# Attention and two dense layers on one core: the products of two pairs of heads in one run, and the keys' exponential one step earlier

## The chip, the cores and the metric

The kernel runs on one core of one Trainium2 chip. The metric is the device time of one execution in microseconds; the kernel before was run three times. One further execution was taken by the hardware profiler, and all rows shown below come from that one.

## The reference

All arithmetic is in fp32. Attention here has no score matrix: queries are normalized along the 64 features of a head, keys along the 576 positions, and the output is `softmax(q) @ (softmax(k)^T @ v)`, for 8 batches of 8 heads. Then come two dense layers over 4608 tokens.

```python
q_s = softmax(q, axis=-1)             # along the 64 features
k_s = softmax(k, axis=2)              # along the 576 positions
kv  = einsum('bhsd,bhse->bhde', k_s, v)     # 64 x 64 for each head
x   = einsum('bhsd,bhde->bhse', q_s, kv)    # then heads side by side: 4608 x 512
h   = x @ moe_w_in;  x = (h - tanh(h)) @ moe_w_out          # 512 -> 2048 -> 512
h   = x @ moe2_w_in; g = P(h) / (Q(h) + 1e-6)               # cubic over quadratic
out = g @ moe2_w_out
```

## The kernel before

**Blocks and steps.** The 4608 tokens are cut into nine blocks of 512 (`NB`). The first dense layer takes 16 steps a block (`KF`), 144 steps `n` in all. In a step TensorE (PE) makes `first_product`: 12 matmuls of 128x128 by 128x512 into a PSUM tile `hps`, and `second_product1` for the step two before: 12 matmuls into the four `acc` banks. Between the two stand a tanh (ACT, L947), `g = h - tanh(h)` (DVE, L950), and the split of `g` into a high part (ACT, L336) and a low part (POOL, L340). A second stage does the second dense layer after step 143, from about 898 us on; the change does not touch it.

**Attention rides along.** While block `j-1` is in the first dense layer, the attention of block `j` is made in small pieces that are put into the steps by hand. `put(s, fn, j, p)` hangs a piece on step `s`; `p` counts the four pairs of heads, and `first(j)` is the first step of block `j-1`. A plain function runs at the head of its step (`front`), ahead of `first_product`. A tuple of two runs in two places: the first function after the step's dense products (`turn`), the second after the split of `g` (`follow`). Batches have 576 positions and blocks 512, so keys and values of batch `b = j` are made for block `j`.

**Keys of one pair** (`KV_LATER`): `kv_max` and `kv_squares` (DVE: maximum over positions, a transposition, a second maximum, a small result `kd` sent to DRAM), `kv_fetch` (SP: `kd` back, broadcast to all partitions), `kv_join` (DVE, L539), `kv_sub` (DVE, L481), `kv_exp` (ACT, L491), `kv_mm` (PE, L499: 10 matmuls of 128x64 by 128x65, which the trace shows as 20 instructions), and `kv_norm`: `kv_sum` (DVE, L506 and L507) and `kv_parts` (ACT, L513: the result into `bd`).

**Queries of one pair** (`Q_LATER`): `q_max` (DVE, L570), `q_sub` (POOL), `q_exp` (ACT, L585), `q_sum` (DVE, L590 to L592, and POOL), `q_squares` (DVE, L610, and a DMA to DRAM), `q_fetch` (SP, L619: four DMAs back, transposed), `q_mm` (PE, L637: matmuls of 64x64, in two PSUM banks), and `q_out` (ACT, L649: four copies into `xr`). At the last step of a block `next_x` splits `xr` into `xh` (ACT, L320) and `xl` (DVE, L322) for the next block's `first_product`.

**Where the products lie.** Counted from `first(j)`, `q_mm` of the four pairs is at steps 4, 8, 11 and 14. `kv_mm` of pair `p` is at the step of `q_mm` of pair `p-1` and writes the free half of that pair's first bank (`room`); pair 0 is two steps ahead of the block, where the last `q_mm` of the block before is. So PE has four runs of attention products a block. Each pair's keys have `kv_join` and `kv_sub` one step ahead of `kv_mm`, and `kv_exp` at the head of the step of `kv_mm`.

**PSUM and buffers.** `ps_h` has two banks, both used in turn by `hps`; `ps_a` has two banks for the attention. In SBUF the pool `att` holds, by `LATER`, two buffers of `qr`, `qe`, `qm`, `qs` and `rs`, and one of everything else.

**Errands.** At the end of each step, after `follow`, generators advance by one piece: they prepare the second layer's weights (`errands`: ACT L131, L133 and L221, DVE, POOL, DMAs) and the first layer's result (`x2_units`: ACT L365, POOL, DMAs). They share ACT's and SP's queues with the attention.

Of the kernel before, what the change touches and what calls it, by code (L numbers as in the profile page):

```python
# [8 lines left out]
F32 = mybir.dt.float32  # L9
# [5 lines left out]
AF = mybir.ActivationFunctionType  # L15
# [3 lines left out]
P = 128  # L19
NB = 512  # L20
NEG = -3.0e38
EPS_S = 1e-9
# [21 lines left out]
def attention_moe_moe2_kernel(ctx, tc, q, k, v, w1, w2, w3, w4, ca, cb, out):  # L44
# [8 lines left out]
    B, H, S, D = q.shape  # L53
# [13 lines left out]
    bdp = tc.alloc_tile_pool(name="bdp", bufs=1, side="right")  # L67
# [122 lines left out]
    HALF = NB // 2  # L190
# [124 lines left out]
    xr = xp.tile([P, KC, NB], F32, tag="xr", name="xr")  # L315
# [39 lines left out]
    def x2_units(j, k0, k1, ta, tb, free):  # L355
# [35 lines left out]
    absb = const.tile([P, 2], F32, name="absb")  # L391

    bd = {
        (par, p): bdp.tile([P, 2, D], F32, tag=f"bd{par}{p}", name=f"bd{par}{p}")
        for par in range(2) for p in range(NPAIR)
    }
    HEADS = slice(0, D), slice(D, P)
    G = -(-S // P)
    REST = S - (G - 1) * P

    FIRST = {"qr": 4, "ke": 4, "qe": 4, "mx": 2, "mc": 2, "qm": 4, "qs": 4, "rs": 4, "qh": 2}
    LATER = {"qr": 2, "qe": 2, "qm": 2, "qs": 2, "rs": 2}
# [38 lines left out]
    kv_state = {}  # L441
# [47 lines left out]
    def kv_exp(b, p):  # L489
        e = kv_state[b, p]  # L490
        ACT.activation(out=e, in_=e, func=AF.Exp)  # L491

    def kv_mm(b, p, room=None):
        e, vs = kv_state.pop((b, p)), vt.pop((b, p))
        pool, tag = (ps_h, "h") if b == 0 and p >= 2 else (ps_a, "a")
        ps = pool.tile([P, NB], F32, tag=tag, name="kvps") if room is None else room
        for g in range(G):
            for h in range(2):
                PE.matmul(  # L499
                    ps[HEADS[h], HALF:HALF + D + 1], e[:, g, h, :], vs[:, h, g, :], start=g == 0, stop=g == G - 1  # L500
                )
        kv_state[b, p] = ps

    def kv_sum(b, p):
        rs = att_tile(b, [P, 1], F32, "rs")
        DVE.tensor_scalar_add(rs, kv_state[b, p][:, HALF + D:HALF + D + 1], EPS_S)  # L506
        DVE.reciprocal(rs, rs)  # L507
        kv_state[b, p] = kv_state[b, p], rs

    def kv_parts(b, p):  # L510
        ps, rs = kv_state.pop((b, p))
        for h, r in enumerate(HEADS):
            ACT.activation(out=bd[b % 2, p][r, h], in_=ps[r, HALF:HALF + D], func=AF.Copy, scale=rs[r])  # L513

    def kv_norm(b, p):
        kv_sum(b, p)
# [12 lines left out]

    def kv_fetch(b, p):  # L530
        d = kv_state[b, p].rearrange("p c -> (p c)")
        t = att_tile(b, [P, G, 2, D], F32, "ke").rearrange("p g h d -> p (g h d)")[:, 0:NB]
        SP.dma_start(out=t, in_=d.unsqueeze(0).to_broadcast([P, NB]))
        kv_state[b, p] = t

    def kv_join(b, p):
# [2 lines left out]
        DVE.tensor_reduce(out=mx.rearrange("p (c i) -> p c i", i=SQ), in_=rows, axis=AX.X, op=ALU.max)  # L539
        kv_state[b, p] = mx  # L540

    KV_LATER = (kv_max, kv_squares, kv_fetch, kv_join, kv_sub, kv_exp, (kv_mm, kv_norm))
    KV = (kv_max, (kv_turn, kv_top), (kv_back, kv_sub), kv_exp, (kv_mm, kv_norm))

    def spans(j):

        got = []
        at = j * NB
        while at < (j + 1) * NB:
            b = at // S  # L550
# [55 lines left out]

    def q_squares(j, p):
        e = q_state[j, p].rearrange("p g d -> p (g d)")
        t = att_tile(j, [P, 4, 2, D], F32, "qe").rearrange("p g h d -> p (g h d)")
        DVE.transpose(out=t, in_=e)  # L610
        d = dp.tile([P, NB], F32, tag=f"qd{j}{p}", name=f"qd{j}{p}")
        SP.dma_start(out=d, in_=t)
        q_state[j, p] = d
# [8 lines left out]
    def q_mm(j, p):  # L622
        t = q_state[j, p]
        if j == 0:
            ps = ps_acc.tile([P, NB], F32, tag=f"acc{p}", name="xps")
            for h, r in enumerate(HEADS):
                PE.matmul(ps[r], bd[0, p][:, h], t, start=True, stop=True)
            q_state[j, p] = ps
            return
        ps = [ps_a.tile([P, NB], F32, tag="a", name="xps") for _ in range(2)]  # L630
        for b, p0, p1 in sorted(spans(j), key=lambda x: x[2] - x[1]):
            for to in range(2):
                for h, r in enumerate(HEADS):
                    def cols(a):
                        return a.rearrange("x (g p) -> x g p", p=P)[:, :, p0:p1]

                    PE.matmul(  # L637
                        cols(ps[h][HEADS[to], 0:HALF]), bd[b % 2, p][r, h], cols(t[r, to * HALF:(to + 1) * HALF]),
                        start=True, stop=True,
                    )  # L640
        q_state[j, p] = ps
        return ps[0]

    def q_out(j, p):
        ps = q_state.pop((j, p))
        if j > 0:
            for to in range(2):
                for h, r in enumerate(HEADS):
                    ACT.copy(out=xr[r, p, to * HALF:(to + 1) * HALF], in_=ps[h][HEADS[to], 0:HALF])  # L649
        else:  # L650
            ACT.copy(out=xh[:, p, :], in_=ps)
            DVE.tensor_tensor(out=xl[:, p, :], in0=ps, in1=f32(xh[:, p, :]), op=ALU.subtract)
# [9 lines left out]
    def turn(todo):  # L662

        got, room = [], None
        for fn, args in todo:
            if isinstance(fn, tuple):
                room = fn[0](*args, *([room] if room is not None and fn[0] is kv_mm else []))
                got.append(lambda fn=fn, args=args: fn[1](*args))
        return got

# [8 lines left out]
    def put(s, fn, *args):  # L679
        work[max(s, 0)].append((fn, args))  # L680

    def first(j):
        return (j - 1) * KF

    kv_at = {(1, p): 3 * p + 3 for p in range(NPAIR)}
    q_at = {(1, p): (6, 9, 12, 14)[p] for p in range(NPAIR)}
    for j in range(2, NBLK):
        for p in range(NPAIR):
            q_at[j, p] = first(j) + (4, 8, 11, 14)[p]
            if j < B:  # L690
                kv_at[j, p] = q_at[j, p - 1] if p else first(j) - (2 if j > 2 else 0)
    q_from = {(j, p): 3 * p if j == 1 else at - 7 for (j, p), at in q_at.items()}
    for j in range(1, NBLK):
        for p in range(NPAIR):
            if j < B:
                for fn, s in zip(KV, (-3, -2, -1, 0, 0)) if j == 1 else zip(KV_LATER, (-4, -4, -2, -1, -1, 0, 0)):
                    put(kv_at[j, p] + s, fn, j, p)
            s = q_from[j, p]
            steps = (s - 1, s, s + 1, s + 2, s + 4, q_at[j, p]) if j == 1 else (s - 1, s, s + 1, s + 2, s + 3, s + 5, s + 7)
            for fn, s in zip(Q if j == 1 else Q_LATER, steps):  # L700
                put(s, fn, j, p)
        for p in range(2, NPAIR + 2):
            to, before = (j + p // NPAIR, p % NPAIR), (j + (p - 2) // NPAIR, (p - 2) % NPAIR)
            if to in kv_at:
                put(kv_at[before], load_k, *to)
                put(kv_at[before] + 1, load_v, *to)
            if to in q_at:
                put(q_from[before] + 2, load_q, *to)

    with tc.manual_schedule():  # L710
# [200 lines left out]
        for n in range(STEPS):  # L911
            j, f = n // KF, n % KF
# [76 lines left out]
        steps = {f"P{m}": lambda i, m=m: product(i, m) for m in UNITS}  # L989
# [51 lines left out]
```

## Time and profile before

| | |
|---|---|
| median of 3 runs | 1680.5 us (1680.35 to 1681.47) |
| the profiled execution's own time | 1678.42 us |
| its span, first to last instruction | 1676.4 us |
| PE busy | 1622.7 us (97%) |
| DVE, ACT, POOL busy | 1113.0, 1039.4, 1036.3 us |
| granted TensorE clock, mean | 0.996 |

The profiled execution took 2.0 us more than its span, for what lies ahead of the first and behind the last instruction. Busy PE time is a modelled figure: matmuls overlap, and what a matmul costs is read from the distance of its start to the next one's. Among the dense products of the first layer this distance is 0.23 us.

### The profile page before, as it was taken

Reading aid. Unit: us, or ns where it says so; the run is one execution under the profiler, and the core shown is the slowest. Engines: PE = TensorE matmul, PEld = TensorE weight load, DVE = VectorE, ACT = ScalarE, POOL = GpSimd, SP = SyncE. Lnnn points to the kernel's source line nnn. Section 1 sums busy time; section 2 is a strip of 40 time slices with the busy share of each in tenths; the row PEclk is TensorE's granted clock in tenths of the full one; section 3 lists DMA queues with packets and bytes.
Section 4 is the critical chain, followed back from the end, with each engine's and each line's share of the span. In section 5 each row is a group of like instructions: output and inputs, shape, how many; then the busy total and the mean of one; then the engine's idle time right before and its main releaser. Section 6 shows DMA issues by size and latency. Waiting matters only on the chain.

```text
span 1676.4 us, 26996 instructions
## 1 busy us (share of the span) xinstructions
PE 1622.7 (97%) x9400; PEld 1373.3 (82%) x9400; DVE 1113.0 (66%) x1840; ACT 1039.4 (62%) x1893; POOL 1036.3 (62%) x875
## 2 busy tenths in 40 slices
PE   5889999999999999999999999999999999999998
PEld 3667778778878788788887999898989898999996
DVE  7987556566655655453213778787878787878787
ACT  5676454555545555454324777777777777777775
POOL 4222637365463736364343888888888777888876
PEclk9999999999999999999999999999999999999999
DMA  8553665747465564633188576767676666666640
GB/s 235 169 168 96 176 180 156 208 143 208 143 197 151 175 187 143 198 115 112 48 304 305 196 255 223 252 235 254 233 256 228 247 215 247 215 249 216 212 148 26
DMA packets 250728, 323.75 MB, mean 193 GB/s; under 512 B 119008, under 2 KB 185568, under 8 KB 241376
## 3 DMA queue, kind: packets, MB, share of 16 engines
q1 hardware_dynamic: 250592, 322.03, 59.9%
q8 instruction: 74, 1.21, 0.3%
q14 instruction: 62, 0.51, 0.1%
HBM read 249.04 MB, written 72.93 MB: 192 GB/s over the span
## 4 chain that ended last, share of the span: by engine, by line
PE 75%; DVE 8%; DMA 6%; ACT 5%; SPq 3%; issue 2%; POOL 0%; DVEq 0%; ACTq 0%; POOLq 0%
PE acc L80 13%; PE acc L81 13%; PE acc L82 12%; PE z L835 11%; PE y L835 8%; PE hps L80 5%; PE hps L81 5%; PE hps L82 5%; DMA u<-x2d 2%; SPq L619 1%; DMA ke<-kd 1%; DMA xh<-x2d 1%; PE xps L499 1%; ACT m L133 1%; DVE mx L457 1%
## 5 line engine op out<-in xcount | busy, mean ns | idle before, releaser
L340 POOL TENSOR_TENSOR gl<-t,gh 128x512 fp32r<-128x512 f32 x128 | 175.1, 1368 | 305.3 <-ACT gh L336 279.7
L336 ACT CAST gh<-t 128x512 fp32r<-128x512 f32 x128 | 79.6, 622 | 269.3 <-PE acc L82 132.4
L892 POOL TENSOR_TENSOR n<-n,r 128x512 f32<-128x512 f32 x144 | 186.3, 1294 | 97.4 <-ACT r L889 92.0
L950 DVE TENSOR_TENSOR t<-hps,t 128x512 f32<-128x512 f32 x128 | 88.0, 688 | 229.8 <-ACT t L947 229.8
L892 POOL TENSOR_TENSOR n<-n,n 128x512 f32<-128x512 f32 x144 | 186.7, 1296 | 36.2 <-ACT n L876 36.2
L892 POOL TENSOR_TENSOR n<-n,h 128x512 f32<-128x512 f32 x144 | 187.3, 1300 | 9.6 <-DMA xl<-x2d 9.6
L947 ACT ACTIVATE t<-hps 128x512 f32<-128x512 f32 x144 | 85.9, 597 | 110.8 <-PE hps L82 74.5
L846 ACT COPY sums<-z 128x256 f32<-128x256 f32 x144 | 53.8, 373 | 134.5 <-PE z L835 134.5
L872 ACT ACTIVATE n<-h,coef 128x512 f32<-128x512 f32 x144 | 116.6, 810 | 0.3 <-POOL n L892 0.3
L902 DVE CAST gh<-a 128x512 fp32r<-128x512 f32 x144 | 99.6, 692 | 15.8
L905 DVE TENSOR_TENSOR gl<-a,gh 128x512 fp32r<-128x512 f32 x144 | 99.6, 692 | 15.2 <-DVE gh L902 0.5
L881 DVE SCALAR_TENSOR_TENSOR a<-h,absb,a 128x512 f32<-128x512 f32 x144 | 107.6, 747 | 3.0 <-ACT a L866 2.9
L898 DVE SCALAR_TENSOR_TENSOR a<-a,n 128x512 f32<-128x512 f32 x144 | 100.0, 694 | 13.9 <-POOL n L892 8.0
L866 ACT ACTIVATE a<-h,coef 128x512 f32<-128x512 f32 x144 | 100.5, 698 | 3.1 <-DVE gl L905 3.1
L895 DVE SCALAR_TENSOR_TENSOR a<-a,r 128x512 f32<-128x512 f32 x144 | 99.4, 690 | 0.8 <-ACT r L889 0.8
L884 ACT ACTIVATE r<-a,bias_q 128x512 f32<-128x512 f32 x144 | 97.1, 674 | 0.0
L889 ACT ACTIVATE r<-r 128x512 f32<-128x512 f32 x144 | 91.1, 632 | 4.6
L869 ACT ACTIVATE h<-h 128x512 f32<-128x512 f32 x144 | 89.2, 620 | 1.0 <-DVE h L857 0.8
L593 POOL TENSOR_TENSOR qe<-qe,qs 128x512 f32<-128x512 f32 x36 | 42.7, 1186 | 47.9 <-DVE qs L592 47.9
L853 DVE TENSOR_TENSOR h<-y,sums 128x256 f32<-128x256 f32 x72 | 30.6, 425 | 58.1 <-PE y L835 58.1
L857 DVE TENSOR_TENSOR h<-y,top 128x512 f32<-128x512 f32 x72 | 49.7, 690 | 27.8 <-ACT top L846 25.8
L80 PE MATMUL hps<-xh,wa0h 128*128 128x512 f32 x144 | 57.5, 399 | 3.9 <-DVE gl L340 3.9
(293 smaller groups left out, 5129.7 us busy)
## 6 DMA issues: line engine op xcount, KB each, us to landing
u<-x2d SPq DMA_DIRECT2D x78, 256.0 KB, 5.5
raw<-in_moe_w_in_dram SPq DMA_DIRECT2D x32, 512.0 KB, 4.5
raw<-in_moe_w_out_dram SPq DMA_DIRECT2D x32, 512.0 KB, 4.1
x2d<-raw SPq DMA_DIRECT2D x64, 256.0 KB, 3.0
x2d<-xr SPq DMA_DIRECT2D x56, 256.0 KB, 3.8
wa0h<-wa0d SPq DMA_DIRECT2D x9, 1024.0 KB, 5.3
wa1h<-wa2d SPq DMA_DIRECT2D x9, 1024.0 KB, 5.1
wa2h<-wa4d SPq DMA_DIRECT2D x9, 1024.0 KB, 5.0
```

Of the source, the lines that this page charges most:

```text
L80: PE.matmul(o, lhi, rhi, start=start, stop=False)
L81: PE.matmul(o, lhi, rlo, start=False, stop=False)
L82: PE.matmul(o, llo, rhi, start=False, stop=stop)
L340: eng.tensor_tensor(out=gl, in0=g, in1=f32(gh), op=ALU.subtract)
L835: PE.matmul(o, w, x[:, xc], start=m in (1, 5) and c == k == 0, stop=c == 1 and k == 2, skip_group_check=True,)
L866: ACT.activation(out=new(t, "a", ps_a), in_=t["h"], func=AF.Abs, scale=b0)
L872: ACT.activation(out=new(t, "n1"), in_=t["h"], func=AF.Identity, scale=a3, bias=a2)
L881: DVE.scalar_tensor_tensor(out=t["a"], in0=t["h2"], scalar=b1, in1=t["a"], op0=ALU.mult, op1=ALU.add)
L892: return lambda t: POOL.tensor_tensor(out=t[a], in0=t[a], in1=t[b], op=op)
L898: DVE.scalar_tensor_tensor(out=t["a"], in0=t["a"], scalar=2.0, in1=t["n0"], op0=ALU.subtract, op1=ALU.mult)
L902: DVE.tensor_copy(out=t["g"][0], in_=t["a"])
L905: DVE.tensor_tensor(out=t["g"][1], in0=t["a"], in1=f32(t["g"][0]), op=ALU.subtract)
```

## The change

The steps of the products are moved together: `q_mm` of pairs 0 and 1 at step 8 of the block, of pairs 2 and 3 at step 14; `kv_mm` of pairs 2 and 3 at step 8, of the next block's pairs 0 and 1 at step 14 (for `j = 2` at its step 2). The pieces ahead of them follow: for even pairs the queries' pieces run from three steps further ahead of their product, the keys' from one step further. `q_mm` of two pairs shares two banks, one half of each for each pair, and `q_out` copies both pairs with four copies of 64x512 instead of eight of 64x256. The keys' products of two pairs (from batch 2 on) share one bank of `ps_h`, at columns 0 and 128. `kv_exp` becomes the second function of a tuple whose first does nothing: it runs in `follow` of the step of `kv_sub`. For odd batches `bd` holds 64 columns and is written by one ACT instruction instead of two. `ke` and `qh` get two buffers; `kr` and `qt` are new single buffers for what used to take one of `ke` and `qe`.

```diff
@@
     bd = {
-        (par, p): bdp.tile([P, 2, D], F32, tag=f"bd{par}{p}", name=f"bd{par}{p}")
+        (par, p): bdp.tile([P, 2 - par, D], F32, tag=f"bd{par}{p}", name=f"bd{par}{p}")
         for par in range(2) for p in range(NPAIR)
     }
+    def bd_of(b, p, h):
+        return bd[b % 2, p][HEADS[h], 0 if b % 2 else h]
-    LATER = {"qr": 2, "qe": 2, "qm": 2, "qs": 2, "rs": 2}
+    LATER = {"qr": 2, "qm": 2, "qs": 2, "rs": 2, "ke": 2, "qh": 2}
@@ def kv_mm
-        ps = pool.tile([P, NB], F32, tag=tag, name="kvps") if room is None else room
+        at = HALF
+        if b > 1:
+            at = p % 2 * P
+            if not at:
+                shared["kv"] = ps_h.tile([P, NB], F32, tag="h", name="kvps")
+            ps = shared["kv"]
+        elif room is None:
...
+        ps = ps[:, at:at + D + 1]
@@ def kv_parts
-        for h, r in enumerate(HEADS):
-            ACT.activation(out=bd[b % 2, p][r, h], in_=ps[r, HALF:HALF + D], func=AF.Copy, scale=rs[r])
+        if b % 2:
+            ACT.activation(out=bd[1, p][:, 0], in_=ps[:, 0:D], func=AF.Copy, scale=rs)
+        else:
+            for h, r in enumerate(HEADS):
+                ACT.activation(out=bd[0, p][r, h], in_=ps[r, 0:D], func=AF.Copy, scale=rs[r])
@@ def kv_fetch
-        t = att_tile(b, [P, G, 2, D], F32, "ke").rearrange("p g h d -> p (g h d)")[:, 0:NB]
+        t = att_tile(b, [P, NB], F32, "kr")
@@
-    KV_LATER = (kv_max, kv_squares, kv_fetch, kv_join, kv_sub, kv_exp, (kv_mm, kv_norm))
+    KV_LATER = (kv_max, kv_squares, kv_fetch, kv_join, kv_sub, (nothing, kv_exp), (kv_mm, kv_norm))
@@ def q_squares
-        t = att_tile(j, [P, 4, 2, D], F32, "qe").rearrange("p g h d -> p (g h d)")
+        t = att_tile(j, [P, 4, 2, D], F32, "qt").rearrange("p g h d -> p (g h d)")
@@ def q_mm
-        ps = [ps_a.tile([P, NB], F32, tag="a", name="xps") for _ in range(2)]
+        at = p % 2 * HALF if j > 1 else 0
+        if not at:
+            shared["q"] = [ps_a.tile([P, NB], F32, tag="a", name="xps") for _ in range(2)]
+        ps = shared["q"]
@@ def q_out
+            if j > 1 and p % 2 == 0:
+                return
+            n = 2 if j > 1 else 1
             for to in range(2):
                 for h, r in enumerate(HEADS):
-                    ACT.copy(out=xr[r, p, to * HALF:(to + 1) * HALF], in_=ps[h][HEADS[to], 0:HALF])
+                    ACT.copy(
+                        out=xr[r, p + 1 - n:p + 1, to * HALF:(to + 1) * HALF],
+                        in_=ps[h][HEADS[to], 0:n * HALF].rearrange("p (c x) -> p c x", c=n),
+                    )
@@
-            q_at[j, p] = first(j) + (4, 8, 11, 14)[p]
+            q_at[j, p] = first(j) + (8, 8, 14, 14)[p]
             if j < B:
-                kv_at[j, p] = q_at[j, p - 1] if p else first(j) - (2 if j > 2 else 0)
-    q_from = {(j, p): 3 * p if j == 1 else at - 7 for (j, p), at in q_at.items()}
+                kv_at[j, p] = first(j) + (8 if p > 1 else 2 if j == 2 else -2)
+    q_from = {(j, p): 3 * p if j == 1 else at - (7 if p % 2 else 10) for (j, p), at in q_at.items()}
+    kv_from = {(b, p): at - (1 if b == 1 or p % 2 else 2) for (b, p), at in kv_at.items()}
...
-                for fn, s in zip(KV, (-3, -2, -1, 0, 0)) if j == 1 else zip(KV_LATER, (-4, -4, -2, -1, -1, 0, 0)):
-                    put(kv_at[j, p] + s, fn, j, p)
+                s, at = kv_from[j, p], kv_at[j, p]
+                steps = (s - 2, s - 1, s, at, at) if j == 1 else (s - 3, s - 3, s - 1, s, s, s, at)
+                for fn, s in zip(KV if j == 1 else KV_LATER, steps):
+                    put(s, fn, j, p)
-            steps = (s - 1, s, s + 1, s + 2, s + 4, q_at[j, p]) if j == 1 else (s - 1, s, s + 1, s + 2, s + 3, s + 5, s + 7)
+            steps = (s - 1, s, s + 1, s + 2, s + 4, at) if j == 1 else (s - 1, s, s + 1, s + 2, s + 3, s + 5, at)
...
-                put(kv_at[before], load_k, *to)
+                put(kv_from[before] + 1, load_k, *to)
```

## Rows read from the trace of the kernel before

**Rows 1.** Windows: stretch, length, busy PE, PEld, DVE, ACT, POOL (instructions), clock, DMA.

```profile
118.00:128.00 10.00, 7.43 (x62) 5.47 (x62) 9.69 (x19) 5.76 (x11) 2.34 (x2) 1.00 0.42 135
...
160.00:898.00 738.00, 728.24 (x3901) 591.08 (x3900) 372.24 (x607) 352.11 (x673) 369.57 (x299) 1.00 0.57 169
```

**Rows 2.** Timeline of PE around one run: start, length, line, what, count.

```profile
463.93 0.39 PE L82 MATMUL acc<-gh,wb0l 128*128 128x512 f32 x1
464.25 0.67 PE L637 MATMUL xps<-qh,bd 64*64 64x96 f32 x16
464.84 0.80 PE L499 MATMUL xps<-vt,ke 128*64 128x65 f32 x20
465.57 0.50 PE L80 MATMUL hps<-xh,wa1h 128*128 128x512 f32 x1
465.91 0.40 PE L81 MATMUL hps<-xl,wa1h 128*128 128x512 f32 x1
```

**Rows 3.** The same run, timelines of stretches inside it: first start, those left.

```profile
464.46 0.45 PE L637 MATMUL xps<-qh,bd 64*64 64x160 f32 x8
...
464.60 0.32 PE L637 MATMUL xps<-qh,bd 64*64 64x160 f32 x4
...
465.01 0.64 PE L499 MATMUL xps<-vt,ke 128*64 128x65 f32 x16
...
465.19 0.46 PE L499 MATMUL xps<-vt,ke 128*64 128x65 f32 x10
```

**Rows 4.** Chain that ended last, a run without keys: start, time until next.

```profile
748.72 0.59 PE xps L637 x8
```

**Rows 5.** Waits from 160 to 830 us: in total, times, longest.

```profile
DVE rs L506 <- ACT xr L649: 54.1, 23, 3.8
...
DVE mx L539 <- DMA ke<-kd: 51.4, 16, 5.8
...
PE xps L499 <- ACT ke L491: 9.2, 8, 2.1
PE hps L81 <- DVE xl L322: 0.5, 1, 0.5
```

**Rows 6.** Chain that ended last, 473 to 491 us.

```profile
476.39 4.73 DMA ke<-kd
...
483.73 1.23 DVE mx L457
...
485.61 0.61 DVE t L950
...
486.82 0.66 ACT e L131
...
489.14 0.65 ACT ke L491
```

**Rows 7.** Windows, just behind the run at 177 us; columns as in Rows 1.

```profile
181.10:184.50 3.40, 3.40 (x9) 2.64 (x8) 1.69 (x4) 3.28 (x9) 2.93 (x3) 0.50 1.06 314
```

**Rows 8.** Timelines at a step 8 and a step 14; wait in brackets.

```profile
482.03 0.39 PE L80 MATMUL hps<-xh,wa2h 128*128 128x512 f32 x1
...
487.56 0.67 PE L637 MATMUL xps<-qh,bd 64*64 64x96 f32 x16
...
490.81 0.69 DVE L950 TENSOR_TENSOR t<-hps,t 128x512 f32<-128x512 f32 x1 [4.23 <-ACT t L947]
...
335.57 0.69 DVE L950 TENSOR_TENSOR t<-hps,t 128x512 f32<-128x512 f32 x1 [3.71 <-ACT t L947]
335.85 0.67 PE L637 MATMUL xps<-qh,bd 64*64 64x96 f32 x16
```

**Rows 9.** The tile xps: duration ns min/median/max, first and last start.

```profile
L649 ACT COPY xr<-xps x128: 358/368/377, 87.7 to 807.4; 64x256 f32<-64x256 f32 x128
L513 ACT ACTIVATE bd<-xps,rs x52: 309/310/312, 89.3 to 700.6; 64x64 f32<-64x64 f32 x52
...
L651 ACT CAST xh<-xps x4: 586/586/591, 25.4 to 36.7; 128x512 fp32r<-128x512 f32 x4
```

More of the change, by code (lines that the diff above doesn't have):

```diff
@@ L491, in kv_exp @@
         ACT.activation(out=e, in_=e, func=AF.Exp)
+    shared = {}
     def kv_mm(b, p, room=None):
         e, vs = kv_state.pop((b, p)), vt.pop((b, p))
-        pool, tag = (ps_h, "h") if b == 0 and p >= 2 else (ps_a, "a")
-        ps = pool.tile([P, NB], F32, tag=tag, name="kvps") if room is None else room
+        at = HALF
[5 more added lines that the diff above has]
+        elif room is None:
+            pool, tag = (ps_h, "h") if b == 0 and p >= 2 else (ps_a, "a")
+            ps = pool.tile([P, NB], F32, tag=tag, name="kvps")
+        else:
+            ps = room
+        ps = ps[:, at:at + D + 1]
         for g in range(G):
             for h in range(2):
-                PE.matmul(
-                    ps[HEADS[h], HALF:HALF + D + 1], e[:, g, h, :], vs[:, h, g, :], start=g == 0, stop=g == G - 1
-                )
+                PE.matmul(ps[HEADS[h]], e[:, g, h, :], vs[:, h, g, :], start=g == 0, stop=g == G - 1)
         kv_state[b, p] = ps
@@ L505, in kv_sum @@
         rs = att_tile(b, [P, 1], F32, "rs")
-        DVE.tensor_scalar_add(rs, kv_state[b, p][:, HALF + D:HALF + D + 1], EPS_S)
+        DVE.tensor_scalar_add(rs, kv_state[b, p][:, D:D + 1], EPS_S)
         DVE.reciprocal(rs, rs)
@@ L511, in kv_parts @@
         ps, rs = kv_state.pop((b, p))
-        for h, r in enumerate(HEADS):
-            ACT.activation(out=bd[b % 2, p][r, h], in_=ps[r, HALF:HALF + D], func=AF.Copy, scale=rs[r])
+        if b % 2:
+            ACT.activation(out=bd[1, p][:, 0], in_=ps[:, 0:D], func=AF.Copy, scale=rs)
+        else:
+            for h, r in enumerate(HEADS):
+                ACT.activation(out=bd[0, p][r, h], in_=ps[r, 0:D], func=AF.Copy, scale=rs[r])
     def kv_norm(b, p):
@@ L540, in kv_join, with nothing @@
         kv_state[b, p] = mx
-    KV_LATER = (kv_max, kv_squares, kv_fetch, kv_join, kv_sub, kv_exp, (kv_mm, kv_norm))
+    def nothing(b, p):
+        pass
+    KV_LATER = (kv_max, kv_squares, kv_fetch, kv_join, kv_sub, (nothing, kv_exp), (kv_mm, kv_norm))
     KV = (kv_max, (kv_turn, kv_top), (kv_back, kv_sub), kv_exp, (kv_mm, kv_norm))
@@ L637, in q_mm @@
                     PE.matmul(
-                        cols(ps[h][HEADS[to], 0:HALF]), bd[b % 2, p][r, h], cols(t[r, to * HALF:(to + 1) * HALF]),
+                        cols(ps[h][HEADS[to], at:at + HALF]), bd_of(b, p, h), cols(t[r, to * HALF:(to + 1) * HALF]),
                         start=True, stop=True,
@@ L666, in turn @@
             if isinstance(fn, tuple):
-                room = fn[0](*args, *([room] if room is not None and fn[0] is kv_mm else []))
+                given = fn[0](*args, *([room] if room is not None and fn[0] is kv_mm else []))
+                room = given if fn[0] is q_mm else room
                 got.append(lambda fn=fn, args=args: fn[1](*args))
@@ L695, in attention_moe_moe2_kernel @@
             if j < B:
-                for fn, s in zip(KV, (-3, -2, -1, 0, 0)) if j == 1 else zip(KV_LATER, (-4, -4, -2, -1, -1, 0, 0)):
-                    put(kv_at[j, p] + s, fn, j, p)
-            s = q_from[j, p]
-            steps = (s - 1, s, s + 1, s + 2, s + 4, q_at[j, p]) if j == 1 else (s - 1, s, s + 1, s + 2, s + 3, s + 5, s + 7)
+                s, at = kv_from[j, p], kv_at[j, p]
+                steps = (s - 2, s - 1, s, at, at) if j == 1 else (s - 3, s - 3, s - 1, s, s, s, at)
+                for fn, s in zip(KV if j == 1 else KV_LATER, steps):
+                    put(s, fn, j, p)
+            s, at = q_from[j, p], q_at[j, p]
+            steps = (s - 1, s, s + 1, s + 2, s + 4, at) if j == 1 else (s - 1, s, s + 1, s + 2, s + 3, s + 5, at)
             for fn, s in zip(Q if j == 1 else Q_LATER, steps):
```

## The prediction

> **What bounds the kernel now.** I read the windows first. From 160 to 898 us, the steps of the first layer behind its slow start, PE is busy 728 of 738 us and no other engine much over half the time [rows 1]. PE's own stream sets the end of this stage: the dense products, and what stands between them. The timeline of PE shows that: a run of attention products, drawn out at both of its ends [rows 2, 3]. The waits name the only other holes: PE waits 9.2 us in 8 places for the keys' exponential, and 0.5 us for `xl` [rows 5]. The chain shows why that exponential was late [rows 6], and a window that one such wait also cost clock [rows 7]. The second stage starts when the last block's products are done, and moves with them.
>
> **What a run costs.** Dense matmuls start 0.23 us apart. Into the run the distance is 464.25 - 463.93 = 0.32, 0.09 more. The queries' part takes 0.59 to the keys' first start, the keys' part 0.73, and the first dense matmul behind it is followed after 0.34, 0.11 more [rows 2]. Sum, with roundings, 1.53. Queries alone take 0.59 too [rows 4], with the ends 0.79; keys alone 0.09 + 0.73 + 0.11 = 0.93. From step 16 on there are 23 runs of both (24 pairs of keys of batches 2 to 7, the first without queries), one of keys alone and five of queries alone: 35.2 + 0.9 + 4.0 = 40.1 us.
>
> **A second pair in the same run.** Once the part is under way, six keys' instructions start within 465.19 - 465.01 = 0.18 us, so a pair's 20 take 0.59. Four queries' instructions of 160 columns take 464.60 - 464.46 = 0.14 [rows 3], four of 96 columns 0.08 in proportion; a pair has two fours of each, 0.44. The trace shows no second pair behind a first. Bounds: at most the whole 0.59 and 0.73 again, so that only the ends are saved; at least this streaming pace. I take the latter, as the nearest row: within a part, too, each instruction brings new weights. A merged run then costs 1.53 + 0.44 + 0.59 = 2.56, two pairs of queries alone 1.23, two of keys alone 1.52. After the change there are 11, three and one of these: 28.2 + 3.7 + 1.5 = 33.4 us. Gain **6.7**; by the upper bounds 14 runs fewer with ends of 0.2, 2.8.
>
> **The exponential's place.** In the case of rows 6 the keys' fetch took 4.73 us. DVE then did join, subtraction, a transposition, and the next pair's `kv_max` with its two followers, 485.61 - 483.73 = 1.9 us, before L950. ACT did the high part of `g`, then four errands from 486.82 on, and only at 489.14 the exponential. In `follow` it stands ahead of these errands: 2.3 us earlier. The mean wait is 9.2 / 8 = 1.2 us and the longest 2.1 [rows 5], so this alone covers them. At step 7 the 1.9 us of the next `kv_max` are gone as well (it is at step 4 now), and the keys' products come 0.44 us later in a run. I count all **9.2** as gained; bounds 0, if the fetch is what is late, and 9.2. The fetch stays close: DVE waits 51.4 us for it in 16 joins, up to 5.8 [rows 5]. `kr` is a single buffer, so an odd pair's fetch now waits on SP for the even pair's `kv_join`; queued behind it are the errands' stores and the loads of keys and values. Issued as a step begins, 4.73 us bring it in before the next one, 5.4 us later.
>
> **Clock.** Behind the run at 177 us, where a wait lay in front of the keys' products, the granted clock was 0.50 (1.2 GHz) for 3.4 us with nine matmuls [rows 7]; at 0.23 their eight distances would take 1.8. Gain **1.6** if that wait goes; else 0.
>
> **ACT and `next_x`.** Four copies of 64x512 replace eight of 64x256. The nearest row is one of 128x512, 0.59 against 0.37 [rows 9]: 2.4 us instead of 2.9 for two pairs. But they come together, 2.4 instead of 1.5 at step 14, with `bd` two to four times 0.31 instead of twice, and the next block's first `q_exp` (128x512, so some 0.6) moves into step 15, ahead of `next_x`. Against this the copies no longer wait for the keys, whose bank was the queries', and start 1.2 us before the run ends; and three DVE instructions of `q_sum` leave step 15. Today `next_x` costs PE 0.5 us [rows 5]. I take a loss of **0.6** over six blocks; bounds -0.5, and +9 if ACT comes 1.5 later each time.
>
> **The keys' bank.** DVE's read of the key sums waits 54.1 us in 23 cases, up to 3.8, for ACT's copies out of other columns of the same bank [rows 5]. Now two pairs' sums and `bd` share one bank. ACT's copies end 1.2 us behind the run and four `bd` take 1.2; with one more wait of the mean size (54.1 / 23 = 2.4) between the two pairs that makes 4.8, without it 2.4. The bank's next user is the product after next, 5.5 us (24 matmuls) behind the run, so I take nothing; bounds 0, and at the longest wait 6.2 - 5.5 = 0.7 in each of 11 runs. The Trainium skill, "PSUM — Partial Sum Buffer", section "PSUM bank collisions raise a hardware error", has two engines kept apart by bank and quadrant, two readers too. The trace's wait agrees; by that rule the sum would still be mine at the mean wait, and 7.7 us worse at the longest.
>
> **One bank less for `hps`.** In a run's step the keys hold the second bank of `ps_h`, so the next `first_product` needs the one whose `hps` L950 has just read. At a step 8 the product began at 482.03 and the run at 487.56; with a merged run the next product would begin 5.53 + 2.47 = 8.0 us after the step did. L950 ended at 491.50, 9.5 after it; at a step 14 it ended at 336.26, inside its run [rows 8]. The 9.5 held the 1.9 of `kv_max`: 7.6 without. I take **0.5** for a late one; bounds 0, and 1.5 at each of six steps 8.
>
> **The slow start.** DVE is full between 118 and 128 us, 19 instructions in 9.69 us, 0.5 each [rows 1]. For batch 2 four of them (2 us) leave step 12 for 13, three (1.5) enter step 14, five (2.5) leave step 15. I take 0; bounds -2.5 and +2. What remains (`bd` of odd batches in one instruction, `qt`, later loads of values) lies in steps where ACT, POOL and SP have room: ACT is busy 352 of 738 us [rows 1]. Without that cover the `bd` instructions would give 0.31 each.
>
> **Sum.** -6.7 - 9.2 - 1.6 + 0.6 + 0.5 = -16.4. The profiled execution took 1678.4 us (its span of 1676.4 and 2.0 around it), which gives 1662.0; the median of the runs lies 2.1 above it, so **1664**.
>
> **Rivals.**
> *The waits stay.* The fetch is what is late, not ACT's order. For it: DVE's 51.4 us. Against: behind the fetch of rows 6 came 8 us of other work, most of which is moved. 6.7 - 1.1 = 5.6 gained: 1675; with half of the waits gone, 1669.5. Chance 0.13.
> *Nothing saved inside a run.* Each pair pays its fill again: 2.8 + 9.2 + 1.6 - 1.1 = 12.5 gained, 1668. Chance 0.08.
> *The keys' bank is held too long*, by the wait above at its longest: 16.4 - 7.7 gained, 1672. Chance 0.04.
> *The missing bank of `hps` decides: slower.* PE stands behind each merged run until L950 is done. At 16.4 / 11 = 1.5 us a run the gain is eaten; with L950 ending 11.3 us after its step's start it is 3.3 a run, 36 in all: 1700. For it: the 9.5. Against: step 14, where L950 ends before the run does. Chance 0.05.
> *The clock falls behind each merged run*, as behind that at 177 us: 11 times 1.6 eats 17.6: 1682, no change. Against: over the whole stage the clock is 1.00 [rows 1], so of 29 runs, 8 of them with a wait inside, hardly another lowered it. Chance 0.04.
> My forecast has 0.66.
>
> **Numbers.** The forecast alone: 1660 to 1668. The range goes on to the first three rivals, 1659.5 to 1675, and leaves out the last two and tails. A measurement of this kernel cannot tell under 0.2% (3.4 us) from no change. Faster 0.66 + 0.13 + 0.08 + 0.04, less tails: 0.89; same 0.06; slower 0.05.
>
> **What would show it.** Right: 15 runs from step 16 on, those of both kinds 2.5 to 2.6 us; no wait of PE for L491; the clock 1.00 in the first steps of block 1; the second stage some 16 us earlier. Wrong: waits for L491 that stay; `hps` waiting for L950, or for L513, behind runs; 0.43 instead of 0.23 between dense matmuls behind them; waits for `xl` of over 1 us at block ends; the first layer's block 1 beginning later.

## The result, and the profile after

The changed kernel takes 1664.4 us (median of four runs, 1662.8 to 1665.1), the kernel before in the same session 1681.0: a ratio of 0.9898, 95% interval 0.9886 to 0.9911. Forecast were 1664 and a range of 1659.5 to 1675. The profiled execution took 1664.0 us with a span of 1662.3, so 14.1 less span than before, where the sum of the prediction had 16.4. That the median fits to half a microsecond is partly luck: the profiled execution before lay 2.1 us below its median, this one 0.4.

First the windows of the changed kernel, with the columns of [rows 1]:

```profile
118.00:128.00 10.00, 9.22 (x42) 7.22 (x41) 9.73 (x20) 7.89 (x15) 2.34 (x2) 1.00 0.41 117
160.00:898.00 738.00, 735.58 (x4012) 604.90 (x4011) 372.27 (x614) 345.92 (x622) 375.28 (x304) 1.00 0.59 176
```

PE is busy 735.6 of 738 us, where it was 728.2 [rows 1]: the holes are gone. The waits from 160 to 830 us, as in [rows 5]:

```profile
DVE mx L556 <- DMA kr<-kd: 25.5, 15, 3.8
...
DVE rs L520 <- ACT bd L530: 10.4, 6, 3.4
DVE rs L520 <- ACT bd L527: 10.0, 6, 3.0
...
PE hps L80 <- DVE rs L520: 0.8, 1, 0.8
...
PE hps L80 <- DVE t L983: 0.2, 1, 0.2
PE hps L81 <- DVE xl L322: 0.2, 1, 0.2
```

No wait for the keys' exponential (L495 now) is left. PE waits 1.0 us for a bank of `hps` and 0.2 for `xl`. (The 0.8 stands under L520, but that is the instruction right behind L983 on DVE: L983, which reads the bank, ends at 205.63 us and the product starts at 205.69.) DVE still waits for the keys' fetch, 25.5 us where it was 51.4 [rows 5]. Next, PE's timeline around a merged run, one of eleven:

```profile
388.19 0.39 PE L82 MATMUL acc<-gh,wb1l 128*128 128x512 f32 x1
388.51 1.10 PE L660 MATMUL xps<-qh,bd 64*64 64x128 f32 x32
389.54 1.39 PE L515 MATMUL kvps<-vt,ke 128*64 128x65 f32 x40
390.86 0.50 PE L80 MATMUL hps<-xh,wa2h 128*128 128x512 f32 x1
391.19 0.39 PE L81 MATMUL hps<-xl,wa2h 128*128 128x512 f32 x1
```

Read as in [rows 2], the entry is 388.51 - 388.19 = 0.32, the queries take 1.03, the keys 1.32, and the next dense product starts 0.33 behind the first: with 0.23 taken off each end, 2.55 us. The prediction had 0.59 + 0.44 = 1.03 and 0.73 + 0.59 = 1.32.

**Where the 14.1 us came from.** I cut the spans by the first dense product of steps 12, 16 and 143 in PE's timeline, and add up what each run of attention products costs beyond the dense products around it.

| us | before | after | difference |
|---|---|---|---|
| start to step 12 | 118.4 | 122.0 | +3.6 |
| start to step 16 | 148.4 | 151.4 | +3.0 |
| step 16 to step 143 | 745.0 | 727.5 | -17.5 |
| of it: runs, without waits inside | 41.1 (29 runs) | 34.6 (15 runs) | -6.5 |
| of it: waits inside runs | 9.2 | 0 | -9.2 |
| of it: dense products at half clock | 1.6 | 0 | -1.6 |
| step 143 to the end | 783.0 | 783.4 | +0.4 |

The 34.6 holds 1.1 us of waits for the bank of `hps` at the ends of two runs. The steady stage gave more than the 16.4 of the sum. The slow start, which the prediction had at nothing, took 3.0 of it back in this pair of profiles.

### The profile page after: what moved, and what is told of

Read it like the earlier page. It is cut to its first block, busy times and chain, and to the rows that moved or that the text cites. A ratio compares the mean times of both kernels' runs of the same rounds, so it can differ in the third digit from the quotient of the medians.

```text
span 1662.3 us, 26919 instructions
## 1 busy us (share of the span) xinstructions
PE 1615.2 (97%) x9400; PEld 1374.6 (83%) x9400; DVE 1105.1 (66%) x1840; ACT 1023.0 (62%) x1821; POOL 1036.5 (62%) x875
## 4 chain that ended last, share of the span: by engine, by line
PE 82%; DVE 6%; DMA 4%; ACT 3%; issue 1%; POOL 1%; SPq 1%; DVEq 0%; POOLq 0%; ACTq 0%
PE acc L80 14%; PE acc L81 14%; PE acc L82 14%; PE z L868 12%; PE y L868 9%; PE hps L80 6%; PE hps L82 6%; PE hps L81 6%; DMA u<-x2d 2%; PE xps L660 1%; PE kvps L515 1%; DMA xh<-x2d 1%; ACT m L133 1%; DMA kr<-kd 1%; DVE m L134 1%
## 5 line engine op out<-in xcount | busy, mean ns | idle before, releaser
L983 DVE TENSOR_TENSOR t<-hps,t 128x512 f32<-128x512 f32 x128 | 88.0, 688 | 234.8 <-ACT t L980 234.7
L980 ACT ACTIVATE t<-hps 128x512 f32<-128x512 f32 x144 | 85.8, 596 | 120.3 <-PE hps L82 85.0
L595 POOL TENSOR_TENSOR qe<-qr,qm 128x512 f32<-128x512 f32 x36 | 43.1, 1198 | 38.1 <-PE qps L619 29.0
```

## The experiments

The medians of the kernel before lay at 1681.0 to 1683.5 us in the sessions, so kernels are compared by their ratio to it. Where an edit touches one stage, the stages of the table above, read from one profile of each kernel, show more than the whole time.

**The same two kernels again.** One further profile each, for the spread.

> The kernel before once more, for the spread of the slow start: step 16 began at 148.4 us. If the slow start varies between executions by 2 us and more, it begins at 150 us or later here or in the next run; else within 0.5 us of 148.4, and 151.4 in the next.

> The changed kernel once more, for the spread of the slow start: step 16 began at 151.4 us. Displaced pieces: within 0.5 us of that again. Spread: 149 to 153. The runs behind step 16 cost 2.55 us each again, and PE waits under 0.5 us for L495.

Measured: spans of 1679.1 and 1664.4 us. Step 12 began at 118.5 and 121.7, step 16 to 143 took 745.7 and 727.3: these stages repeat within 0.8 us. Step 16 began at 149.5 and 151.1. So the kernel before fits neither of its cases: behind a wait of 2.25 us at step 12, which stands in its first profile too, 12 dense products started 0.43 us apart, at the lower clock, where in the first profile they started 0.23 apart. The start is thus longer by 3.0 us in one pair of profiles and by 1.6 in the other; up to step 12, ahead of that clock, it is longer by 3.6 and 3.3, which is no accident. The end did not repeat: 783.9 and 786.0 from step 143 on, where the first profiles had 783.0 and 783.4. Behind step 16 PE had no wait for L495, and nine of the eleven merged runs cost 2.55 or 2.56 us again.

**The exponential alone, in the kernel before.**

```diff
+    def nothing(b, p):
+        pass
+
-    KV_LATER = (kv_max, kv_squares, kv_fetch, kv_join, kv_sub, kv_exp, (kv_mm, kv_norm))
+    KV_LATER = (kv_max, kv_squares, kv_fetch, kv_join, kv_sub, (nothing, kv_exp), (kv_mm, kv_norm))
...
-                for fn, s in zip(KV, (-3, -2, -1, 0, 0)) if j == 1 else zip(KV_LATER, (-4, -4, -2, -1, -1, 0, 0)):
+                for fn, s in zip(KV, (-3, -2, -1, 0, 0)) if j == 1 else zip(KV_LATER, (-4, -4, -2, -1, -1, -1, 0)):
```

> The kernel before, with only the keys' exponential moved: second function of a tuple in the step of kv_sub, as in the change; products stay in four runs a block. If ACT's order made the exponential late: it comes 2.3 us earlier, PE's waits for L491 behind 160 us fall from 9.2 us to under 2, the half-clock stretch at 181 us goes, and the time is 1669 to 1672. If the fetch from DRAM made it late: at least half of the waits stay, and the time is 1676 to 1681.

Measured: 1679.9 us, ratio 0.9992 (0.9981 to 1.0003): no change. The waits from 160 to 830 us:

```profile
DVE mx L539 <- DMA ke<-kd: 56.0, 17, 5.8
...
PE xps L499 <- ACT ke L491: 8.1, 5, 3.8
```

Of the 9.2 us of waiting 8.1 are still there, in fewer and longer pieces. The longest two show why. SP's timeline of this kernel around 666 us:

```profile
665.75 2.69 SPq L622 DMA_DIRECT2D qh<-qd  x4
668.48 0.62 SPq L533 DMA_DIRECT2D ke<-kd  x1
```

The same of the kernel before:

```profile
665.88 2.69 SPq L619 DMA_DIRECT2D qh<-qd  x4
668.62 0.62 SPq L533 DMA_DIRECT2D ke<-kd  x1
```

And PE's timeline of this kernel, the run that needs these keys:

```profile
675.84 0.73 PE L640 MATMUL xps<-qh,bd 64*64 64x32 f32 x16
...
679.49 0.80 PE L499 MATMUL xps<-vt,ke 128*64 128x65 f32 x20 [2.92 <-ACT ke L491]
```

The fetch is issued at the same time in both, within 0.14 us, behind the four of the queries. In the kernel before the queries of this run began at 677.4; here PE is there 1.6 us earlier and waits 2.92 us instead of 1.78. The step behind the run begins at 680.2 instead of 680.7. In block 1 it is plainer still: the step that holds the run begins 3.6 us earlier (195.0 for 198.6), its fetch is issued 0.6 later (193.3 for 192.8), its wait grows from 0.2 to 3.8, and the next step begins at 205.73 in this kernel and 205.72 in the kernel before. What was gained was given back at the next place where the fetch, and not PE, sets the time. Nor does the move bring 2.3 us everywhere: at a step 8 of block 4 the exponential starts 1.6 us earlier (487.41 for 489.04) and its wait is gone, but behind the fetch at 668 us only one errand, L365, stood ahead of it, and it starts 0.4 earlier (678.70 for 679.13). It still stands behind the next pair's `kv_max` and L950 there. Both long waits also cost clock; the window behind that at 676 us (columns as in [rows 1]):

```profile
680.00:684.00 4.00, 4.00 (x20) 3.17 (x17) 1.21 (x4) 3.11 (x8) 2.81 (x3) 0.61 0.76 202
```

**The exponential back, in the changed kernel.**

```diff
-    KV_LATER = (kv_max, kv_squares, kv_fetch, kv_join, kv_sub, (nothing, kv_exp), (kv_mm, kv_norm))
+    KV_LATER = (kv_max, kv_squares, kv_fetch, kv_join, kv_sub, kv_exp, (kv_mm, kv_norm))
...
-                steps = (s - 2, s - 1, s, at, at) if j == 1 else (s - 3, s - 3, s - 1, s, s, s, at)
+                steps = (s - 2, s - 1, s, at, at) if j == 1 else (s - 3, s - 3, s - 1, s, s, at, at)
```

> The changed kernel, with the exponential back at the head of the step of its product; products merged. If the merging also helps the exponential (kv_max gone from step 7, the keys' products later in a run): PE waits 2 to 5 us for it, 1666 to 1670. If ACT's order alone counts: the 9 us of waits and the clock are back, 1674 to 1676. If the order does not count: 1664 to 1665.

Measured: 1665.0 us, 0.9903 (0.9888 to 0.9918), the same as the changed kernel; no wait of PE for the exponential. Its place is worth nothing here either. ACT's timeline of this kernel at a step 8, the errands ahead of both pairs' exponential:

```profile
480.50 0.59 ACT L221 CAST e<-m 128x512 fp32r<-128x512 f32 x1
480.99 0.61 ACT L365 CAST raw<-xr 128x512 fp32r<-128x512 f32 x1
481.51 1.36 ACT L495 ACTIVATE ke<-ke 128x640 f32<-128x640 f32 x2
```

And its PE:

```profile
482.94 1.10 PE L660 MATMUL xps<-qh,bd 64*64 64x96 f32 x32
483.97 1.39 PE L515 MATMUL kvps<-vt,ke 128*64 128x65 f32 x40
```

The exponentials end at 482.87, 1.1 us before the keys' products start, although they stand behind the errands as before.

**Only `kv_max` earlier, in the kernel before.** Pair 3's maximum and its two followers go from step 7, where pair 2's join stands, to step 6.

```diff
-                    put(kv_at[j, p] + s, fn, j, p)
+                    put(kv_at[j, p] + s - (j > 1 and p == 3 and fn in KV_LATER[:2]), fn, j, p)
```

> The kernel before with one piece moved: kv_max and kv_squares of pair 3 at step 6 of the block instead of step 7, where they stand between kv_join of pair 2 and L950. New theory (the exponential is late because DVE's queue at step 7 is: the fetch from DRAM, then 1.9 us of kv_max, then L950, and ACT's high part and exponential behind it): L950 of step 7 ends up to 1.9 us earlier, the waits for L491 (9.2 and 10.0 us in the two profiles) fall to under 4, and the time is 1672 to 1676. If DVE's queue is not it: waits of 8 us and more, 1679 to 1682.

Measured: 1673.5 us, 0.9949 (0.9935 to 0.9963). The waits from 160 to 830 us:

```profile
DVE mx L539 <- DMA ke<-kd: 47.6, 16, 6.1
...
PE xps L499 <- ACT ke L491: 4.9, 4, 2.6
```

By PE's timeline the runs of step 8 waited 5.3 us before, in five places; now one waits, 0.3. DVE's 1.9 us between join and L950 were what made them late. The 4.6 left stand at steps 4 and 11, which this edit does not touch. The waits did not fall under the 4 us that were expected; the time lies in the range expected. No dense product ran at half clock; step 16 to 143 took 738.7 us, 6.3 less than before.

**Only the fetch earlier, in the kernel before.** It is issued a step sooner, into a tile of its own.

```diff
-        t = att_tile(b, [P, G, 2, D], F32, "ke").rearrange("p g h d -> p (g h d)")[:, 0:NB]
+        t = att_tile(b, [P, NB], F32, "kr")
...
-                for fn, s in zip(KV, (-3, -2, -1, 0, 0)) if j == 1 else zip(KV_LATER, (-4, -4, -2, -1, -1, 0, 0)):
+                for fn, s in zip(KV, (-3, -2, -1, 0, 0)) if j == 1 else zip(KV_LATER, (-4, -4, -3, -1, -1, 0, 0)):
```

> The kernel before with the keys' fetch one step earlier, into a buffer of its own, so that it is no longer issued behind the four fetches of queries of the same step; kv_max stays at step 7. If the fetch is late because of its place on SP: DVE's waits for it (51.4 us) halve at least, waits for L491 fall to under 4 us, 1670 to 1675. If only kv_max counts: waits for L491 of 7 us and more, 1677 to 1682.

Measured: 1667.4 us, 0.9914 (0.9899 to 0.9928): this edit alone brings most of what the whole change does. PE waits for no exponential; DVE's wait for the fetch, 51.4 us before [rows 5], is nearly gone:

```profile
PE hps L81 <- DVE xl L322: 0.5, 1, 0.5
...
DVE mx L539 <- DMA kr<-kd: 0.4, 1, 0.4
```

Step 16 to 143 took 733.5 us, 11.5 less than before, near the 9.2 of waits and 1.6 of clock that were there to gain; the whole time is shorter than was expected. The edit has two parts, but the tile of its own explains little: in the kernel before SP held the fetch back at five of 23 places, for at most 0.8 us, and at none of the eight whose run then waited.

**The change's pieces, but four runs a block.** The pairs' products stand at steps 7, 8, 13 and 14, each with banks of its own as before.

```diff
-        if b > 1:
+        if b > B:
...
-        at = p % 2 * HALF if j > 1 else 0
+        at = 0
...
-            if j > 1 and p % 2 == 0:
-                return
-            n = 2 if j > 1 else 1
+            n = 1
...
-            q_at[j, p] = first(j) + (8, 8, 14, 14)[p]
+            q_at[j, p] = first(j) + (7, 8, 13, 14)[p]
...
-                kv_at[j, p] = first(j) + (8 if p > 1 else 2 if j == 2 else -2)
-    q_from = {(j, p): 3 * p if j == 1 else at - (7 if p % 2 else 10) for (j, p), at in q_at.items()}
-    kv_from = {(b, p): at - (1 if b == 1 or p % 2 else 2) for (b, p), at in kv_at.items()}
+                kv_at[j, p] = first(j) + (8 if p > 1 else 2 if j == 2 else -2) - (1 - p % 2)
+    q_from = {(j, p): 3 * p if j == 1 else at - (7 if p % 2 else 9) for (j, p), at in q_at.items()}
+    kv_from = {(b, p): at - 1 for (b, p), at in kv_at.items()}
```

> The changed kernel with its early exponential and its new order of pieces, but each pair's products in a run of its own, in neighbouring steps (7, 8, 13, 14), in the banks of before. If a run's ends and fills cost what the trace shows: 40.3 us of runs against 33.4, so 6.9 us more than the changed kernel, 1670 to 1672. If the second stage or another engine hides it: under 1667.

And the same with the exponential back at the products' step, as above:

> The changed kernel's order of pieces, but the products in four runs a block (steps 7, 8, 13, 14, in the banks of before) and the exponential back at the head of its product's step: neither merging nor the early exponential. If the order of the pieces took the waits away: PE waits under 1 us for L495, 1670 to 1672, as with the early exponential. If the early exponential counts once the products are not merged: waits of 3 us and more, 1674 to 1678.

Measured: 1670.7 us, 0.9934 (0.9921 to 0.9946), and 1669.4 us, 0.9932 (0.9916 to 0.9948). Neither waits inside a run; 30 runs cost 40.6 us in both, where the changed kernel's 15 cost 34.6. So merging is worth 6.0 us by the runs and 5.7 to 6.1 by the ratios (0.0034 to 0.0036 of 1681). Step 16 to 143 shows less, 732.3 us in both against 727.5, so 4.8: between runs the changed kernel loses 1.4 us, most of it at the starts of blocks 3 and 7, and these two lose nothing there. And without merging and without the early exponential the changed kernel's order of the pieces, with its buffers, already removes every wait.

**Queries and keys in turn inside the merged run.** Pair by pair: queries, keys, queries, keys.

```diff
+        pieces = [x for x in todo if isinstance(x[0], tuple)]
+        if pieces and min(args[0] for _, args in pieces) > 1:
+            for fn, args in sorted(pieces, key=lambda x: x[1][1] % 2):
+                fn[0](*args)
+            return [lambda fn=fn, args=args: fn[1](*args) for fn, args in pieces]
```

> The changed kernel with the products inside a run in another order: queries of one pair, keys of one pair, then queries and keys of the other; still two runs a block. If each change of shape drains PE (0.11 us) and shows the first weights (0.05): two more changes in 11 runs, some 0.32 a run, 3.5 us more, 1667 to 1669, a run 2.8 to 2.9 us. If only the ends against the dense products cost: 1664 to 1665, a run 2.55.

Measured: 1668.9 us, 0.9923 (0.9911 to 0.9936). PE's timeline of one of its runs:

```profile
392.64 0.67 PE L660 MATMUL xps<-qh,bd 64*64 64x128 f32 x16
393.24 0.80 PE L515 MATMUL kvps<-vt,ke 128*64 128x65 f32 x20
393.98 0.67 PE L660 MATMUL xps<-qh,bd 64*64 64x128 f32 x16
394.57 0.80 PE L515 MATMUL kvps<-vt,ke 128*64 128x65 f32 x20
395.31 0.51 PE L80 MATMUL hps<-xh,wa2h 128*128 128x512 f32 x1
```

From 392.64 to 395.31 it is 2.67 us where the same products took 390.86 - 388.51 = 2.35 above: 0.32 for two more changes between tiles of 64x64 and 128x64, 0.16 each. The eleven runs lose 3.5 us by this, and step 16 to 143 takes 731.5 instead of 727.5. The saving lies in the changes of shape, inside the run as at its ends. The Trainium skill, "TensorEngine Tiling (Array Packing)", section "Key Properties", says that a change of tiling mode, unlike a change of tile, empties the engine first. A price of 0.16 us for each change fits that; the trace does not show the emptying itself.

**Ballast on DVE at step 7.** Three reductions of 128x512 in the changed kernel, in six blocks, their result unused.

```diff
+    scrap = const.tile([P, 8], F32, name="scrap")
+
+    def ballast(j, p):
+        for _ in range(3):
+            t = f32(wsl["b", 0][0][:, 0, :]).rearrange("p (g d) -> p g d", d=D)
+            DVE.tensor_reduce(out=scrap, in_=t, axis=AX.X, op=ALU.max)
+
+    for j in range(2, B):
+        put(first(j) + 7, ballast, j, 0)
```

> The changed kernel with three DVE reductions of 128x512 more (0.67 us each, their result unused) at the head of step 7 of six blocks, about what kv_max took there before. New theory: L950 of step 7 ends some 2 us later, the tanh and L950 of step 8 too, and as the merged run's next product needs the bank that L950 reads, PE waits 0.5 to 2 us at each of four to six steps 8, 3 to 8 us in all: 1667 to 1672. If DVE has room there: 1664 to 1665.

Measured: 1666.1 us, 0.9908 (0.9892 to 0.9925), which the whole time can't tell from the changed kernel. The waits from 160 to 830 us can:

```profile
PE hps L80 <- DVE rs L520: 2.7, 3, 1.4
PE hps L80 <- DVE t L993: 1.6, 2, 0.9
PE hps L81 <- DVE xl L322: 0.3, 2, 0.2
```

Some 2 us on DVE ahead of L983 (L993 here) make 4.3 us of waits for the bank of `hps`, behind five runs of step 8, where the changed kernel has 1.0, and step 16 to 143 takes 730.6 us, 3.1 more. The missing bank is a real price, and the changed kernel is nearly clear of it.

**The slow start: batch 2's pieces back.** In the changed kernel the first merged run of batch 2 goes from step 18 to step 20, and its pieces with it.

```diff
-                kv_at[j, p] = first(j) + (8 if p > 1 else 2 if j == 2 else -2)
+                kv_at[j, p] = first(j) + (8 if p > 1 else 4 if j == 2 else -2)
...
+    q_from[2, 0] = 13
+    kv_from[2, 0], kv_from[2, 1] = 15, 18
```

> The changed kernel with batch 2's early pieces back where they were in the slow start: queries of pair 0 one step earlier, keys of pair 0 at steps 12 to 15, keys of pair 1 from step 15, and their products two steps later, at step 20. If the displaced DVE pieces made the slow start 3.0 us longer in the profile after: step 16 begins near 148.4 instead of 151.4 us, time 1661 to 1662.5. If that is the spread between executions: 1664 to 1665, and step 16 begins anywhere between 148 and 152.

Measured: 1664.6 us, 0.9896 (0.9877 to 0.9914); step 12 still begins at 122.4 and step 16 at 151.1. These pieces are not the cause.

POOL's and ACT's waits of the changed kernel from 36 to 152 us point elsewhere:

```profile
POOL qe L595 <- PE qps L619: 29.0, 3, 11.2
...
ACT qe L605 <- POOL qe L595: 6.5, 3, 2.3
```

In the kernel before POOL has no such wait there. The change takes `qe`'s second buffer away (`qe` is gone from `LATER`), and in block 1 a pair's subtraction, L595, must now wait until TensorE has transposed the pair before it, L619. The chain that ended last goes through it:

```profile
113.94 0.45 PE qps L619 x4
...
114.51 1.05 POOL qe L595
...
115.58 0.63 ACT qe L605
116.21 0.49 ACT t L980
...
116.73 0.71 DVE hps L983
```

The queries' exponential stands in ACT's order ahead of L980, the activation of `hps`; it comes late, and DVE and the high part of `g` behind it.

**Two buffers again.** Block 1's odd pairs take the tile `qt`, which stands idle in that block.

```diff
-        e = att_tile(j, [P, 4, 2, D], F32, "qe")
+        e = att_tile(j, [P, 4, 2, D], F32, "qt" if j == 1 and p % 2 else "qe")
```

> The changed kernel, and only block 1's subtraction from the queries is touched: pairs 1 and 3 write into the other tile of queries, which stands idle in block 1, so that the four pairs have two buffers again, as in the kernel before. Theory: the 3 us by which the changed kernel enters step 12 late (121.7 to 123.1 us in all its relatives, 118.4 to 118.8 in the kernel before and its relatives) come from the single buffer, for which POOL's subtraction waits 29.0 us on TensorE's transposes (L619) in the first 152 us. Then that wait is gone or under 5 us, step 12 begins at 118.5 to 119.5 us, step 16 at about 148.5, and the time falls by 2 to 3 us, to 1661.5 to 1662.5. Rival: the transposes are only the last of several things that the subtraction waits for, and the start is late through the different order of the pieces of blocks 1 and 2. Then step 12 stays at 121.5 to 123 and the time at 1664 to 1665.

Measured: 1660.3 us, 0.9864 (0.9847 to 0.9880), the fastest of all, below the changed kernel's interval. The wait for L619 is gone, step 12 begins at 116.55 and step 16 at 148.95, as before the change; step 16 to 143 takes 727.5 as in the changed kernel. The theory's cause holds, and its size was too small: step 12 comes 2 us earlier than was expected, and the time lies below the range. Between steps 12 and 16, 32.4 us against 29.4, 3.0 of the 5.5 gained are lost again. Half of this is waiting, by PE's waits from 116 to 149 us:

```profile
PE hps L82 <- DVE wa3l L158: 5.1, 3, 2.2
```

That is the decoding of weights, for which the changed kernel waits 3.7 us there. The other half is clock, as this window shows (columns as in [rows 1]):

```profile
116.00:122.00 6.00, 3.25 (x9) 2.30 (x10) 5.90 (x13) 4.72 (x9) 2.33 (x2) 0.82 0.41 122
```

Behind the first of these waits, 2.25 us long, eight distances between dense products are 0.39 to 0.43 us instead of 0.23, which makes 1.6 us.

## Why the prediction was right, and where it was not

**What a run costs; a second pair in the same run: right.** 2.55 us for 2.56. The 15 runs sum to 34.6 us; 1.3 of that is the excess of four runs over their like, of which two wait 1.1 for the bank of `hps`; the other 33.3 stand against 33.4. Pieces in four runs against merged ones: 5.7 to 6.1 us for the 6.7, the bank's waits already taken off. The rival by which each pair pays its fill again falls: the interleaved run pays it, and loses.

**The exponential's place: the size right, the reason wrong.** 9.2 us were forecast and 9.2 came. But the step that says "this alone covers them" failed: alone it changed nothing, and taken back it changed nothing. It took the 2.3 us of one case for all, though 0.4 came at the wait of 1.8 us behind the fetch at 668 us, and it took the fetch's time as fixed to PE's steps. The fetch stands in SP's order behind other transfers, and at the two longest waits it kept its absolute time, or came 0.6 later, when PE came earlier. What removed the waits is the order of the pieces. The new buffers alone are an unlikely rival and were not tried: of the eight fetches of keys ahead of runs that waited SP held none back, and the queries' fetch in front of them once, for 0.6 us. Three things in the order come into question.

First, a `kv_max` no longer shares a step with another pair's join. Before, it did at steps 7 and 10; moved from step 7 alone, it took step 8's waits from 5.3 us to 0.3. DVE's timeline of the changed kernel at a step 7, to be held against [rows 6]:

```profile
474.37 1.10 DVE L556 TENSOR_REDUCE mx<-kr 128x128 f32<-128x512 f32 x1 [2.34 <-DMA kr<-kd]
475.50 0.83 DVE L485 TENSOR_TENSOR ke<-kt,mx 128x640 f32<-128x640 f32 x1
476.24 0.68 DVE L983 TENSOR_TENSOR t<-hps,t 128x512 f32<-128x512 f32 x1
```

and its ACT:

```profile
477.01 0.62 ACT L336 CAST gh<-t 128x512 fp32r<-128x512 f32 x1 [3.67 <-DVE t L983]
477.54 0.73 ACT L495 ACTIVATE ke<-ke 128x640 f32<-128x640 f32 x1
```

From the join's start to the exponential's end it is 478.27 - 474.37 = 3.9 us; in the same block before 489.78 - 481.14 = 8.6. The fetch itself is no earlier: issued 5.25 us into step 6 in both kernels.

Second, there are no products at steps 4 and 11 any more, where the rest of the waits stood. Third, the late pair's keys now come behind two pairs' queries and the early pair's keys, 0.44 + 0.59 us later in their step.

Of these the first is shown by its experiment. The kernel with four runs and the exponential back has the first two without the third, in which each pair's keys come behind one pair's queries at most, and it waits nowhere: the third is not needed. The second was not tried alone. The rival "the waits stay" had the right cause, a late fetch (issued a step earlier, it alone ends all waits), and the wrong result, since it held that the change leaves what comes behind the fetch as it is.

**Clock: right.** No dense product at half clock behind step 16 in the changed kernel. Merged runs, 2.35 us of small products, never lowered it; waits of 2.05 [rows 7], 2.9 and 3.8 us inside runs did, though not every long one (below).

**ACT and `next_x`: 0 in the sum for 0.6.** The first steps of blocks 3 and 7 last 0.53 and 0.45 us longer than the others', where the kernel before loses 0.95 at block 3: no change. The kernels with four runs lose nothing at any block, so against them merging costs 1.0 here, and the new order of the pieces gave the 0.95 back.

**The keys' bank: right.** Sums and `bd` do block one another (DVE's 10.4 and 10.0 us for L530 and L527 above), each time up to 3.4 us, and nobody on the path waits: from 160 to 830 us PE waits for neither L527 nor L530. The Trainium skill, "PSUM — Partial Sum Buffer", section "PSUM bank collisions raise a hardware error", which the prediction cites, has two engines that touch the same bank and quadrant kept apart, two readers too. These waits agree.

**One bank less for `hps`: right in kind, 1.1 us for 0.5.** It showed behind one run each of blocks 1 and 2 alone, by 0.9 and 0.2 us; of the 1.0 in the waits above 0.2 has another cause (at 191.35 us, behind no run, PE waits for an L983 that is late through an errand on ACT). The ballast shows how near the rest are.

**The slow start: wrong, +3.0 us where +2 was the worst end** (+1.6 in the second pair of profiles, where half clock lengthens the kernel before). The step that failed is its last: "what remains (`bd` of odd batches in one instruction, `qt`, later loads of values) lies in steps where ACT, POOL and SP have room". It asked what the new tile `qt` costs and not what the buffer given up for it had hidden, and it took the room of POOL and ACT from the steady stage's averages, while block 1 has other pieces (L619 in place of `q_squares`) and a full DVE.

**The sum.** -6.5 - 9.2 - 1.6 - 0.2 in the steady stage, +3.0 and +0.4 around it: -14.1 for -16.4. The forecast of the median was saved by the 1.7 us by which the two profiled executions stand differently to their medians.

Open: how much the second point above did; why the whole time of the last kernel falls by 5.7 us by its ratio where its stages show 3.2 (2.4 in the start, 0.8 in the end, which differs by more than that between executions of one kernel); and whether the queries' four transfers behind which the keys' fetch stands on SP could simply follow it, which was not tried.

## What to carry to other kernels

A wait has a chain behind it, and an edit to its last link can be given back in full unless the first link moves with the engine that waits; ask whether a late transfer is issued relative to that engine's steps or by a queue that keeps its own time, and try the transfer's own place first: here that edit alone brought 14.5 us by its ratio (0.0086 of 1681) and 11.5 in the steady stage, the whole change 17.1 and 17.5. When a change takes a buffer away, list who wrote into it next, in every stage that uses the tile, the start too. Small products of different shapes are best sorted by shape: each change cost 0.16 us in the middle of a run and about 0.1 at each of its ends.

## What the runs showed of the hardware

I had not expected a merged run to come out as the plain sum of what a single run's timeline shows for its fill and its flow, to 0.01 us: 40 keys' products of 128x65 start 0.03 us apart, though each brings weights of its own. Nor that what a wait costs in clock goes so little by its length. In the kernel before a wait of 2.05 us at 179 us is followed by 0.50 [rows 7], in the one with the exponential alone one of 2.9 by 0.61; in the one with only `kv_max` earlier, a wait of 2.6 us at 221 us leaves the clock where it was, as this window shows (columns as in [rows 1]):

```profile
224.00:228.00 4.00, 4.00 (x27) 3.28 (x23) 1.95 (x6) 3.07 (x9) 1.29 (x1) 1.00 0.56 109
```

And at step 12 the kernel before waits 2.25 us in both of its profiles, behind the same products; in the first PE goes on at full clock, in the second 12 products run at half of it. What else PE did ahead of these waits was not compared, so the cause stays open.
